# A decode kernel whose final wait for its two output stores is moved from SP to GpSimd

## The chip, the cores and the metric

The kernel runs on one core of one Trainium2 chip. The metric is the device time of one execution in microseconds (us). Every execution also has a span, from the first to the last recorded instruction. This change is far smaller than 2%, so the document leans on two finer quantities: the time of a run minus its span, and the records of one trace in nanoseconds (ns).

## The reference

One decode step of a transformer layer for a batch of 4: layer norm, attention over the last 4096 positions of a cache (32 query heads, 16 key and value heads of width 128), output projection and residual; then layer norm, a gated feed-forward block of width 4608 and residual. Everything is bf16.

```python
h = x + _A_ref(_layernorm(x, axis=-1), A_k_cache, A_v_cache, A_wq, A_wo)
h2 = h + _B_ref(_layernorm(h, axis=-1), B_W_gate, B_W_up, B_W_down)
return h2                       # 4 x 1 x 576, bf16
```

## The kernel before

The kernel keeps one list of operations for each engine. An operation names what it depends on; at the end each list is written out for its engine, and every dependency becomes a wait on a semaphore. An operation without a function (`None`) is only its waits. It becomes one instruction that waits, which the profile shows as an `EVENT_SEMAPHORE` at the helper's line L110.

```python
    for key, val in need.items():
        if seen.get(key, 0) < val:
            seen[key] = val
            engine.wait_ge(sems[key], val)          # L110
    if o.fn is None:
        continue
```

GpSimd prepares constants at the start (memsets and masks) and has nothing to do afterwards. SP issues every large load. The end of the kernel is this:

```python
dve("OUT0", lambda e: e.tensor_copy(out=out_sb[0:32, :], in_=bank[0][0:32, 0:288]), [("DOWN", 0)])
act("OUT1", lambda e: e.copy(out=out_sb[32:64, :], in_=bank[1][32:64, 0:288]), [("DOWN", 1)])
orow = out.rearrange("b s d -> (b s) d")
for n in range(2):
    P.dma(("sync", "scalar")[n], ("O", n), lambda e, n=n: e.dma_start(     # store n, L712
        out=orow[:, 288 * n:288 * n + 288], in_=out_sb[32 * n:32 * n + 4, :]),
        "d_out", [f"OUT{n}"])
P.op("sync", None, None, [("O", n) for n in range(2)])                     # the final wait
P.emit(nc, es)
```

SP issues one store and ACT the other. Both raise the semaphore `d_out` by 16 when they have landed, and the final wait is for 32.

Of the kernel before, what the change touches and what calls it, by code (L numbers as in the profile page):

```python
# [120 lines left out]
def bass_sequential_preLN__sliding_block_cached__glu_gated_reglu__decode_kernel(  # L121
# [12 lines left out]
    with ExitStack() as es:  # L134
# [5 lines left out]
        P = Prog()  # L140
# [104 lines left out]
        def main_rows(W):  # L245
            return W[0:512, :].rearrange("(p r) n -> p (r n)", r=4)
# [22 lines left out]
        for g, W in ((0, B_W_gate), (1, B_W_up)):  # L269
            for m, n, src in ((4, F // 2, last_rows(W)), (0, 3 * F, main_rows(W)[:, 0:3 * F]), (3, F, main_rows(W)[:, 3 * F:4 * F])):  # L270
                if g == 0 and m == 0:
                    n, src = 4 * F, main_rows(W)
# [438 lines left out]
        for n in range(2):  # L711
            P.dma(("sync", "scalar")[n], ("O", n), lambda e, n=n: e.dma_start(  # L712
                out=orow[:, 288 * n:288 * n + 288], in_=out_sb[32 * n:32 * n + 4, :]),
                "d_out", [f"OUT{n}"])
        P.op("sync", None, None, [("O", n) for n in range(2)])
        P.emit(nc, es)


# [26 lines left out]
```

## Time and profile before

| what | value | where it is read |
|---|---|---|
| time, median of the runs | 378.07 us (378.06, 378.07, 379.07) | the runs |
| span | 376.6 us | page, first line |
| DMA | mean 424 GB/s | page, part 2 |
| chain that ended last | 56% DMA, 21% PE, 20% DVE | page, part 4 |
| last 35 us of the span | one DMA piece of 32.31 us to 374.00 us | chain of waits |
| from the end of SP's wait to the last record of all | 1.461 us | raw trace |

These are lines of the page of the kernel before: its span, the DMA rows of part 2 (40 equal slices of the span) and the head of part 4, the chain that ended last.

```profile
span 376.6 us, 2562 instructions
...
DMA  8999999999999999999999999999999999999996
...
DMA packets 6802, 159.74 MB, mean 424 GB/s; under 512 B 764, under 2 KB 904, under 8 KB 1672
...
DMA 56%; PE 21%; DVE 20%; issue 1%; SPq 1%; ACT 0%
```

The digit 9 in almost every slice says that the DMA engines were busy 90% of the time or more. So the loads fill almost the whole span.

This is the end of the chain of waits of the kernel before, in order of time: start, length (us), what.

```profile
341.69 32.31 DMA sb_arena<-in_B_W_down_dram
374.00 0.04 issue
374.04 0.70 PE psb L705 x6
374.74 0.43 DVE sb_out_sb L708
```

The chain stops at VectorE's cast, at about 375.2 us. Behind it lies the part that this change touches. This is the timeline of the same kernel's tail: start, length (us), engine, line, operation. A `q` after an engine's name stands for its sequencer.

```profile
374.73 0.45 DVE L708 CAST sb_out_sb<-psb 32x288 bf16<-32x288 f32 x1 [9.73 <-PE psb L705]
374.76 0.39 ACT L709 CAST sb_out_sb<-psb 32x288 bf16<-32x288 f32 x1 [9.49 <-PE psb L705]
375.18 0.28 ACTq L712 DMA_DIRECT2D out_dram<-sb_out_sb  x1
375.20 0.34 SPq L712 DMA_DIRECT2D out_dram<-sb_out_sb  x1
```

The final wait is not in this view. It stands in the view of line L110, which gives durations in ns (least, median, most) and the first and last start in us, and in the view of what the SP queue waited for (us in total, times, longest):

```profile
L110 ACTq EVENT_SEMAPHORE  x13: 17/17/556, 20.9 to 334.5; - x13
L110 SPq EVENT_SEMAPHORE  x1: 17/17/17, 376.6 to 376.6; - x1
```

```profile
SPq L110 <- DMA out_dram<-sb_out_sb: 1.0, 1, 1.0
```

SP is done issuing its store and then waits 1.0 us for the stores to land. The 17 ns are only the record of a wait that is already over. The Trainium skill ("Perfetto Trace Analysis", Per-engine timelines, the part on sequencer-only instructions) says the same: the time spent in a semaphore wait is not in the record. This trace agrees for SP's wait, with 17 ns of record for 1.0 us of waiting. It does not agree for an instruction that waits for two semaphores: the longest of ACT's records above, 556 ns from 20.915 us, names two, of which one had its last update at 12.190 us and the other at 21.444 us, 27 ns before the record ended. The wait for the second is inside the record.

What follows the span is in no view, but the raw trace holds the updates of the semaphores. The next fence gives, in ns from the start of the span, the updates of semaphore 2, which no line of the kernel uses. A number in brackets is the step from the update before.

```
kernel before
SP's final wait                              376570 to 376587, end of the span
closing barrier, 9 updates                   374903 375818 375857 375901 376708 376752 376790 376824 376872
                                                    (915)   (39)   (44)  (807)   (44)   (38)   (34)   (48)
235 other semaphores, one update each        376828 to 377467
second barrier, 9 updates                    377691 ... 378048
                                                    (34)   (38)   (44)   (23)   (99)   (38)   (35)   (46)
```

I read each series of nine as a barrier, a place that no engine passes before all five have arrived: one pass over the five engines and back. The fifth update, from which the pass goes back, is called the turn below. The second barrier, where nobody is late, shows the undisturbed steps. The large steps in the first show who was late: the 807 ns end 121 ns after SP's wait. The last update minus 0.18 us is the time of the profiled run (378.048 against 377.87), so what happens behind the span counts in the metric.

### The profile page before, as it was taken

The numbers are of one execution on the slowest core, as the hardware profiler recorded it, in microseconds if no ns is written. First come the engines' busy times: TensorE is split into PE (matmuls) and PEld (weight loads), VectorE is DVE, ScalarE is ACT, GpSimd is POOL, SyncE is SP. The second block draws the span as 40 slices with busy tenths as digits, with TensorE's granted clock in tenths as the row PEclk, the third lists the DMA queues.
The fourth block names the chain that finished last, engine by engine and source line by source line (L and its number), as shares of the span: only waits on it lengthen the run. The fifth ranks groups of instructions, "written<-read, shape, count | busy, mean of one in ns | idle before, by whom it ended". The sixth has DMA issues, their size and how long they took to land.

```text
span 376.6 us, 2562 instructions
## 1 busy us (share of the span) xinstructions
PE 208.8 (55%) x1456; PEld 37.6 (10%) x703; DVE 226.2 (60%) x164; ACT 54.3 (14%) x85; POOL 10.5 (3%) x29
## 2 busy tenths in 40 slices
PE   0304443249919191749282845664655687886674
PEld 0000000001101010001010100100000001002422
DVE  3078888779292959584847777665659423333220
ACT  3193000301000114010101140101010401112010
POOL 8200000000000000000000000000000000000000
PEclk9955888859968797687788796989696968998699
DMA  8999999999999999999999999999999999999996
GB/s 335 446 439 428 416 442 439 428 418 442 437 425 421 439 440 421 421 442 442 425 419 439 442 428 418 438 439 428 425 435 439 423 425 439 422 431 425 437 413 260
DMA packets 6802, 159.74 MB, mean 424 GB/s; under 512 B 764, under 2 KB 904, under 8 KB 1672
## 3 DMA queue, kind: packets, MB, share of 16 engines
q1 hardware_dynamic: 6776, 159.59, 98.8%
q8 instruction: 8, 0.13, 0.1%
q10 hardware_dynamic: 16, 0.01, 0.0%
q14 instruction: 2, 0.02, 0.0%
HBM read 159.58 MB, written 0.00 MB: 424 GB/s over the span
## 4 chain that ended last, share of the span: by engine, by line
DMA 56%; PE 21%; DVE 20%; issue 1%; SPq 1%; ACT 0%
DMA sb_arena<-in_A_k_cache_dram 48%; DVE sb_arena L425 16%; PE psb L34 13%; DMA sb_arena<-in_B_W_down_dram 9%; PE psb L449 4%; PE psb L510 3%; DVE sb_o_tmp L523 1%; DVE sb_pp L488 1%; PE psb L476 1%; SPq L284 0%; DVE sb_pp L471 0%; DVE sb_hx L454 0%; ACT sb_pp L468 0%; PE psb L705 0%; DVE sb_out_sb L708 0%
## 5 line engine op out<-in xcount | busy, mean ns | idle before, releaser
L425 DVE STREAM_TRANSPOSE sb_arena<-sb_arena 128x8192 f32<-128x8192 f32 (+1 forms) x19 | 139.9, 7365 | 66.4 <-DMA sb_arena<-in_A_k_cache_dram 66.4
L449 PE MATMUL psb<-sb_arena 128*32 128x512 bf16 x256 | 44.5, 640 | 118.8 <-DVE sb_arena L425 118.8
L34 PE MATMUL psb<-sb_arena,sb_pp 128*128 128x512 bf16 x382 | 107.3, 389 | 2.9 <-issue 2.8
L510 PE MATMUL psb<-sb_arena,sb_pp 128*128 128x512 bf16 x115 | 44.8, 389 | 8.9 <-DVE sb_o_tmp L523 8.9
L34 PE MATMUL psb<-sb_arena 128*32 128x512 bf16 x256 | 45.4, 645 | 0.0
L520 ACT COPY sb_o_tmp<-psb 32x512 f32<-32x512 f32 x32 | 18.5, 577 | 181.7 <-PE psb L34 181.4
L523 DVE TENSOR_TENSOR sb_o_tmp<-psb,sb_fm 32x512 f32<-32x512 f32 x32 | 21.7, 678 | 18.6 <-PE psb L34 18.1
L449 PEld LDWEIGHTS psb<-sb_arena 128*32 128x32 bf16 x256 | 9.7, 117 | 162.0 <-DVE sb_arena L425 131.8
L510 PEld LDWEIGHTS psb<-sb_arena,sb_pp 128*128 128x128 bf16 x128 | 12.8, 100 | 115.7 <-issue 115.7
L527 DVE TENSOR_REDUCE sb_o_sel<-sb_o_tmp 128x128 f32<-128x512 f32 x16 | 17.7, 1107 | 0.5
L468 ACT ACTIVATE sb_pp<-psb,sb_hx 128x1024 bf16<-128x1024 f32 x4 | 4.5, 1113 | 79.4 <-DVE sb_hx L465 79.4
L488 DVE TENSOR_TENSOR sb_pp<-psb,sb_m 128x1024 bf16<-128x1024 f32 x8 | 9.3, 1206 | 4.6 <-PE psb L476 4.6
L483 ACT ACTIVATE sb_pp<-psb,sb_m 128x512 bf16<-128x512 f32 x16 | 9.8, 698 | 14.6 <-PE psb L476 14.6
L526 DVE TENSOR_TENSOR sb_o_tmp<-sb_o_tmp,sb_fm 64x512 f32<-64x512 f32 x16 | 11.0, 689 | 0.5
L416 ACT COPY sb_arena<-sb_q_keep 32x256 bf16<-32x256 bf16 x8 | 9.7, 1448 | 0.1
L402 DVE CAST sb_pp<-psb 128x512 bf16<-128x512 f32 x1 | 2.4, 2425 | 10.1 <-PE psb L382 10.1
L471 DVE STREAM_TRANSPOSE sb_pp<-sb_pp 128x1024 bf16<-128x1024 bf16 x4 | 5.0, 1245 | 5.1 <-ACT sb_pp L468 5.1
L476 PE MATMUL psb<-sb_pp,sb_to_v 128*32 128x256 bf16 x64 | 4.3, 400 | 6.2 <-DVE sb_pp L471 6.2
L705 PE MATMUL psb<-sb_arena,sb_pp 128*32 128x288 bf16 x72 | 5.4, 288 | 3.8 <-DMA sb_arena<-in_B_W_down_dram 3.8
L708 DVE CAST sb_out_sb<-psb 32x288 bf16<-32x288 f32 x1 | 0.4, 446 | 9.7 <-PE psb L705 9.7
L454 DVE TENSOR_REDUCE sb_hx<-psb 128x1 f32<-128x1024 f32 x4 | 4.9, 1225 | 2.3 <-PE psb L34 2.3
L34 PE MATMUL psb<-sb_arena,sb_hnT 128*32 128x384 bf16 x80 | 6.3, 394 | 0.0
(123 smaller groups left out, 80.4 us busy)
## 6 DMA issues: line engine op xcount, KB each, us to landing
sb_arena<-in_A_k_cache_dram SPq DMA_DIRECT2D x16, 4096.0 KB, 26.1
sb_arena<-in_A_v_cache_dram SPq DMA_DIRECT2D x16, 4096.0 KB, 28.6
sb_arena<-in_A_wo_dram SPq DMA_DIRECT2D x1, 4608.0 KB, 25.3
sb_arena<-in_B_W_gate_dram SPq DMA_DIRECT2D x1, 4608.0 KB, 26.9
sb_arena<-in_A_wq_dram SPq DMA_DIRECT2D x1, 4096.0 KB, 13.1
sb_arena<-in_B_W_down_dram SPq DMA_DIRECT2D x3, 1296.0 KB, 30.9
sb_arena<-in_B_W_up_dram SPq DMA_DIRECT2D x1, 3456.0 KB, 27.8
sb_arena<-in_B_W_up_dram SPq DMA_DIRECT2D x1, 1152.0 KB, 30.3
```

Of the source, the lines that this page charges most:

```text
L34: return e.add_instruction(mybir.InstMatmult(name=e.bass.get_next_instruction_name(), engine=mybir.EngineType.PE, ins=[e.lower_ap(rhs), e. ...
L416: act("QW", lambda e, i=i, q=q: e.copy(out=bass.AP(tensor=arena, offset=32 * i * AW + 2 * i + q, ap=[[AW, 32], [512, 16], [136, 4], [32, 4]]),
L425: dve(("TRA", g), lambda e: e.transpose(out=dst, in_=src), [("L", "K", g)] if lo == 0 else [])
L449: fn = lambda e, out_=out_, lhsT=lhsT, rhs=rhs, start=start, stop=stop: e.matmul(out_, lhsT=lhsT, rhs=rhs, start=start, stop=stop, skip_gr ...
L476: pe(("RM", b, n // 2), lambda e, n=n, i=i: e.matmul(bank[6 if n < 2 else 0][32 * i:32 * i + 32, n % 2 * 256:n % 2 * 256 + 256], lhsT=to_v ...
L483: act(("EV", b, 0), lambda e, a=a: e.activation(out=bass.AP(tensor=pp, offset=2 * a, ap=[[PPW, 128], [8, 2], [32, 128], [1, 2]]), in_=bank ...
L488: dve(("EV", b, 1), lambda e, n=n: e.tensor_tensor(out=bass.AP(tensor=pp, offset=16 + 8 * n, ap=[[PPW, 128], [32, 128], [2, 4], [1, 2]]), ...
L510: fn = lambda e, lhsT=lhsT, rhs=rhs, k=k, j=j: e.matmul(bank[2 + j], lhsT=lhsT, rhs=rhs, start=(k == 0), stop=(k == 7), skip_group_check=True)
L520: act(("OSC", g), lambda e, j=j: e.copy(out=o_tmp[32 * j:32 * j + 32, 0:512], in_=bank[2 + j][32 * j:32 * j + 32, :]), [("PV", g), ("OSEL" ...
L523: dve(("OSD", g), lambda e, j=j: e.tensor_tensor(out=ot(32 * j, 32), in0=bank[2 + j][32 * j:32 * j + 32, :].rearrange("p (t d) -> p t d", ...
L526: dve(("OS", g), lambda e: e.tensor_tensor(out=ot(64, 64), in0=ot(64, 64), in1=fmb(64, 64), op=ALU.mult), [("OSC", g)])
L527: dve(("OSEL", g), lambda e: e.tensor_reduce(out=o_sel[:, qd, b, :], in_=o_tmp[:, 0:512].rearrange("p (t d) -> p d t", d=DH), axis=AX.X, o ...
```

## The change

The final wait leaves SP's list and goes to the end of GpSimd's. It is still the same wait: the kernel may not end before both stores have landed. The diff has no comment; its intent, as I read it, is to let an engine that is idle since 12 us do the waiting, and to end SP's program with its store.

```diff
-        P.op("sync", None, None, [("O", n) for n in range(2)])
+        P.op("gpsimd", None, None, [("O", n) for n in range(2)])
```

No other instruction of any engine moves.

## The prediction

> **What bounds the kernel.** The page's DMA row reads 8 or 9 tenths in nearly every slice, at a mean of 424 GB/s. The chain that ended last is 56% DMA. In the last 40 us it is one DMA piece (the W_down load, 32.31 us to 374.00), then PE 0.70 us and a VectorE cast of 0.43 us to about 375.2. GpSimd works only in the first 12 us (its timeline).
>
> **What the change does.** Every listed instruction keeps its place on its engine. One semaphore wait for both output stores leaves SP's queue and goes behind GpSimd's last memset. Nothing before 375.2 us depends on it, so no load, buffer release or matmul moves.
>
> **The tail, from the raw records of the trace (us from the span's start).**
> - The stores are issued at 375.18 (ACT) and 375.20 (SP).
> - The stores' semaphore counts up until 376.553. SP's wait begins its 17 ns record at 376.570 and the span ends at 376.587.
> - After that, semaphore 2 shows the closing barrier. Its nine updates are at 374.903, 375.818, 375.857, 375.901, 376.708, 376.752, 376.790, 376.824 and 376.872. Then semaphores are reset, and a further barrier ends at 378.048.
>
> The Trainium skill ("Runtime: NRT & Kernel Launch", The ~15µs preamble/postamble breakdown) lists a postamble barrier, reset and barrier, and describes the opening barrier as a serpentine of 8 hops at 44 ns. The trace agrees: nine updates, and hops of 34 to 48 ns where nobody is late. I read the order, as inference from the times, as PE, ACT, GpSimd, VectorE, SP and back. The 807 ns before the fifth update is the wait for SP, at the turn.
>
> **Cost.** Before: from the end of the wait to VectorE's returning update takes 121 + 44 = 165 ns. After: GpSimd is released at the same moment, two places ahead of the turn. It needs its own time to its update, then the hop to VectorE (44 ns), then VectorE out to VectorE back (about 135 ns, from the undisturbed opening barrier: 24 + 111). I estimate GpSimd's own time at 150 ns, from SP's 121 ns plus the some 30 ns by which it seems slower from barrier to first reset. This is 329 ns against 165 ns. So I expect about +0.16 us, all on the critical path.
>
> The runs before are 378.06, 378.07 and 379.07 us, so one run's spread (1 us) is larger than the effect (0.04%).
>
> **Prediction: 378.2 us, 8 in 10 between 377.6 and 379.1. Faster by over 2%: 0.01; within 2%: 0.98; slower by over 2%: 0.01.**
>
> **What would show the steps.** Right: the last record is GpSimd's wait, at 376.6 within the run's own DMA drift; the SP queue has no wait for the output stores; the chain of waits, DMA row and busy times are unchanged; in the barrier's updates the third, not the fifth, is the late one; and from the end of the wait to the last barrier update takes 1.5 to 1.8 us, against 1.46 us now (378.048 - 376.587). Wrong: that tail is unchanged or shorter, or the fifth update is still the late one.
>
> **What could make it wrong.** GpSimd may wake or leave its program more slowly than SP (ACT took 0.354 us from its store issue's end to its update): up to +0.4 us. My reading of the barrier's order may be wrong. Drift of the 375 us of loads by a few tenths can hide or reverse the sign in a median of three. Over 2% would need the loads to move.

## The result

The changed kernel takes 378.50 us (median of 4 runs, 378.44 to 378.65), beside 378.06 us for the kernel before (4 runs, 378.00 to 379.07). The ratio is 1.0006 with a 95% interval of 0.9989 to 1.0023. A ratio is the mean time of one kernel's fast runs over that of the other's of the same rounds, so it is not quite the ratio of the medians: the one run of 379.07 us raises the mean of before.

The same lines of the page of the changed kernel:

```profile
span 376.6 us, 2577 instructions
...
DMA  8999999999999999999999999999999999999996
...
DMA packets 6802, 159.74 MB, mean 424 GB/s; under 512 B 764, under 2 KB 904, under 8 KB 1672
...
DMA 61%; DVE 18%; PE 18%; SPq 1%; issue 0%
```

The span, the DMA row and the rate are as before. The shares of the chain are not quite (DMA 61% against 56%): more of its earlier pieces are loads of the key cache, 53% of the span against 48%. (The 15 more instructions are matmul records, 1471 against 1456, of which a trace can miss some.) The end of its chain of waits has the same steps, 0.05 us later:

```profile
342.56 31.49 DMA sb_arena<-in_B_W_down_dram
374.05 0.04 issue
374.09 0.70 PE psb L705 x6
374.79 0.43 DVE sb_out_sb L708
```

In its view of line L110, SP's row is gone and GpSimd has one. The SP queue's waits contain no line for the output stores any more.

```profile
L110 POOLq EVENT_SEMAPHORE  x1: 17/17/17, 376.6 to 376.6; - x1
```

Nothing in the profile's views is longer, and yet the run is 0.4 us longer. The difference is in the raw records behind the span:

```
kernel after
GpSimd's final wait                          376627 to 376644, end of the span
closing barrier, 9 updates                   374955 375864 377186 377230 377253 377350 377389 377425 377471
                                                    (909) (1322)   (44)   (23)   (97)   (39)   (36)   (46)
second barrier, 9 updates                    378262 ... 378620
```

Now the third update is the late one, and all that follow have the steps of a barrier where nobody else is late. So GpSimd is third, as the prediction had inferred. But its update comes 377186 - 376644 = 542 ns after the end of its wait, where SP's came after 121 ns. From the end of the span to the last update it is 1.976 us instead of 1.461 us: 0.515 us more. Of these, 421 ns are the slower exit (542 against 121), 121 ns the longer way from the third place than from the fifth (285 against 164 ns to the barrier's end), and 27 ns are won back behind the barrier.

### The profile page after: what moved, and what is told of

The parts are those of the page before. It is cut to its first block, busy times and chain, and to the rows that moved or that the text cites. A ratio compares the mean times of both kernels' runs of the same rounds, so it can differ in the third digit from the quotient of the medians.

```text
span 376.6 us, 2577 instructions
## 1 busy us (share of the span) xinstructions
PE 209.9 (56%) x1471; PEld 36.0 (10%) x703; DVE 226.3 (60%) x164; ACT 54.3 (14%) x85; POOL 10.5 (3%) x29
## 4 chain that ended last, share of the span: by engine, by line
DMA 61%; DVE 18%; PE 18%; SPq 1%; issue 0%
DMA sb_arena<-in_A_k_cache_dram 53%; DVE sb_arena L425 16%; PE psb L34 11%; DMA sb_arena<-in_B_W_down_dram 8%; PE psb L449 4%; PE psb L510 3%; DVE sb_o_tmp L523 1%; DVE sb_pp L488 1%; SPq L284 0%; SPq L242 0%; PE psb L476 0%; PE psb L705 0%; DVE sb_out_sb L708 0%; SPq L255 0%; SPq L251 0%
## 5 line engine op out<-in xcount | busy, mean ns | idle before, releaser
L449 PE MATMUL psb<-sb_arena 128*32 128x512 bf16 x256 | 41.6, 625 | 120.8 <-DVE sb_arena L425 120.8
L34 PE MATMUL psb<-sb_arena,sb_pp 128*128 128x512 bf16 x384 | 107.6, 390 | 0.0
L510 PE MATMUL psb<-sb_arena,sb_pp 128*128 128x512 bf16 x128 | 50.6, 395 | 8.9 <-DVE sb_o_tmp L523 8.9
L34 PE MATMUL psb<-sb_arena 128*32 128x512 bf16 x256 | 42.8, 639 | 0.0
L449 PEld LDWEIGHTS psb<-sb_arena 128*32 128x32 bf16 x256 | 8.7, 120 | 163.4 <-DVE sb_arena L425 133.9
L34 PE MATMUL psb<-sb_arena,sb_hnT 128*32 128x384 bf16 x80 | 7.2, 446 | 0.0
L676 DVE TENSOR_TENSOR sb_pp<-psb,sb_pp 128x384 bf16<-128x384 f32 x3 | 1.5, 550 | 8.8 <-PE psb L667 8.8
```

The source lines that it names most:

```text
L34: return e.add_instruction(mybir.InstMatmult(name=e.bass.get_next_instruction_name(), engine=mybir.EngineType.PE, ins=[e.lower_ap(rhs), e. ...
L449: fn = lambda e, out_=out_, lhsT=lhsT, rhs=rhs, start=start, stop=stop: e.matmul(out_, lhsT=lhsT, rhs=rhs, start=start, stop=stop, skip_gr ...
L510: fn = lambda e, lhsT=lhsT, rhs=rhs, k=k, j=j: e.matmul(bank[2 + j], lhsT=lhsT, rhs=rhs, start=(k == 0), stop=(k == 7), skip_group_check=True)
```

## The experiments

Three theories stood at the start.

- **Exit theory**: GpSimd always takes over 0.5 us from its program's last instruction to its update in the closing barrier, and it stands two places ahead of the turn. Both are paid because everything behind the last engine to arrive is serial.
- **Wake theory**: GpSimd was slow because it had been parked in a wait for 364 us.
- **Drift theory**: the difference of the times came from the loads, and the tail had no part in it.

In what follows, "exit" is the time from the end of an engine's last record to its own update in the closing barrier, "tail" is the time from the end of the span to the last update of the second barrier, both from the trace of the profiled run, and "run minus span" is the median over the runs (spans are noted to 0.1 us). The kernel before ran nine times beside each batch: medians 377.96, 378.04 and 377.88 us, and a run minus span of 1.26, 1.26 and 1.27 us. The 95% interval of each ratio is about 0.13% (some 0.5 us) wide to either side, so smaller differences below rest on run minus span and on the records, not on the ratio. Each batch ran on another chip.

### The changed kernel again

No edit.

> The changed kernel again, beside the kernel before on one chip. Tail theory: run time minus span, which was 1.3 us before and 1.8 us after, is again about 0.5 us longer than for the kernel before, and the time is 0.4 to 0.6 us longer. Drift theory (the difference came from the loads): run time minus span is alike and the difference of the times changes size or sign.

Measured: 378.51 us against 377.96 us, ratio 1.0013 (1.0001 to 1.0026). Run minus span is 1.84 us in the median, and lies between 1.81 and 1.84 us in all five runs; for the kernel before it lies between 1.22 and 1.32 us in all nine. Exit 542 ns and tail 1.976 us, the same to the nanosecond as in the first trace. The spans are alike (376.6 to 376.8 us here; 376.5 to 376.7 us before, but for one of 377.3). The drift theory falls: the loss of about 0.55 us is real and lies behind the span. The first comparison showed 0.44 us.

### Both wait

```diff
         P.op("sync", None, None, [("O", n) for n in range(2)])
+        P.op("gpsimd", None, None, [("O", n) for n in range(2)])
```

> The wait is added on GpSimd and kept on SP. If only the engine that is late at the barrier counts, SP's own wait is hidden behind GpSimd's: same time as the changed kernel (about 378.5 us), third barrier update about 540 ns after GpSimd's wait record ends. If taking the wait from SP had itself cost or saved something, the time differs from the changed kernel by over 0.1 us.

Measured: 378.55 us, exit of GpSimd 542 ns, tail 1.974 us. The view of line L110 shows the two waits, which end 8 ns apart:

```profile
L110 SPq EVENT_SEMAPHORE  x1: 17/17/17, 376.8 to 376.8; - x1
L110 POOLq EVENT_SEMAPHORE  x1: 17/17/17, 376.8 to 376.8; - x1
```

So the half of the change that frees SP gains nothing: with SP's wait put back, the time is the changed kernel's. All of the loss is in the half that makes GpSimd wait.

### A second wait on GpSimd, meant to wake it shortly before

```diff
-        P.op("sync", None, None, [("O", n) for n in range(2)])
+        P.op("gpsimd", None, None, ["OUT0"])
+        P.op("gpsimd", None, None, [("O", n) for n in range(2)])
```

> GpSimd waits first for VectorE's output cast (about 375.2 us) and then for the stores, so it has been parked for only some 1.4 us when the stores land. Wake theory (the 542 ns come from having been parked 364 us): the time from its last wait record to its barrier update falls to about 150 ns and the total to about 378.1 us. Exit theory (GpSimd always needs about 540 ns to leave its program): 500 to 580 ns again and about 378.5 us.

```profile
L110 POOLq EVENT_SEMAPHORE  x1: 42/42/42, 376.6 to 376.6; - x1
```

Measured: 378.59 us. The record ends at 376.673 us and the update is at 377.216 us: 543 ns. But the edit did not do what it was meant to do. GpSimd has one record and not two; it names both semaphores, begins at 376.631 us, 24 ns after the last landing of the stores, and lasts 42 ns. The cast had been over since 375.242 us. If it had woken GpSimd for a second wait inside this instruction, the record should hold that wait of some 1.4 us, as ACT's record of 556 ns held its second wait. So this run shows no early waking, and it leaves the wake theory open. The two runs below in which SP waits and GpSimd works decide it.

### The wait on ACT

```diff
-        P.op("sync", None, None, [("O", n) for n in range(2)])
+        P.op("scalar", None, None, [("O", n) for n in range(2)])
```

> The wait is on ACT, second in my reading of the barrier's order. Position and exit theory: the second update is the late one, the third and fourth follow it by 39 and 44 ns, the turn takes about 24 + 100 ns; the time is longer than the kernel before by its place (two hops of about 40 ns, the hop to SP and a turn some 60 ns longer, about 0.1 to 0.15 us) plus what ACT's own exit exceeds SP's 121 ns. If ACT leaves as fast as SP: about 378.2 us; if it needs the 354 ns seen after its store issue: about 378.5 us.

Measured: 378.04 us (before: 377.96), run minus span 1.40 us, tail 1.581 us. The second update is the late one, as the order said, and the exit is 109 ns. ACT stands farther from the turn than GpSimd and still costs only about 0.1 us, so the place explains little; the exit does. The 354 ns from the end of ACT's store issue to its update, which the prediction had taken as a warning, are not what ACT needs after a wait; whether they belong to leaving right behind a store issue is not tested.

### The wait on VectorE

The same edit with `"vector"`.

> The wait is on VectorE, one place before the turn in my reading. The fourth barrier update is the late one; the fifth follows 24 ns and the sixth 97 ns later. If VectorE leaves its program as fast as SP and ACT (121 and 109 ns), the tail from the end of the wait to the last barrier update is 1.50 to 1.58 us and the time 0.05 to 0.15 us over the kernel before. If a slow exit is common to the compute engines and ACT is the exception, the tail is about 1.9 us.

Measured: the fourth update is the late one, exit 147 ns, tail 1.534 us: as expected. The time, 378.31 us against 378.04 us, is not: 0.27 us longer, and run minus span is 1.60 us. The profiled run (379.26 us, in a span that was itself 1 us longer) ended 0.05 us after the last barrier update, where all the other traces so far, before and after included, have it 0.17 to 0.18 us before that update. About 0.23 us lie outside everything that the barrier's records show. One of the later experiments takes this up.

### The wait on PE

The same edit with `"tensor"`.

> The wait is on PE, first in my reading: the first update is the late one and all others follow it at 34, 38, 44, 24, 97, 38, 35 and 47 ns. Place theory: 34 ns more than on ACT plus the difference of the exits. PE's exit is not known; from its 196 ns between the end of its last matmul and its update I expect 100 to 250 ns, so a tail of 1.61 to 1.76 us and a time of 0.15 to 0.35 us over the kernel before. About 1.6 us of tail would say PE leaves like ACT.

Measured: 378.21 us against 378.04 us, the first update is the late one, exit 192 ns, tail 1.720 us. All inside what was expected.

### GpSimd waits and then works

```diff
-        P.op("sync", None, None, [("O", n) for n in range(2)])
+        pool("end", lambda e: e.memset(warm[:, 0:1], 0.0), [("O", n) for n in range(2)])
```

> GpSimd waits for the stores and then does one memset of a column (98 ns elsewhere). If the 542 ns are counted from GpSimd's last instruction of its program, the third update comes 98 to 160 ns later than in the changed kernel (0.64 to 0.70 us after the wait's end). If they are counted from the wait and a memset hides in them, it stays at about 0.54 us. If the memset has the engine finish what a bare wait leaves to the exit, it shrinks below 0.5 us.

This is the memset in the timeline of that run; the bracket says that GpSimd had idled 364.57 us until the stores landed:

```profile
376.77 0.10 POOL L715 MEMSET sb_warm<- 128x1 f32 x1 [364.57 <-DMA out_dram<-sb_out_sb]
```

Measured: the memset ends at 376.873 us and the update is at 377.385 us, 512 ns later, and 659 ns after the stores' last landing (376.726 us), against 583 ns in the changed kernel (376.603 to 377.186). So 76 of the memset's 99 ns are paid on top, and the exit is counted from the last instruction. After a memset it is 30 ns shorter than after a bare wait. The time of 379.06 us (4 runs) doesn't say more, because two of the runs had a span of 377.7 us; run minus span is 1.76 us.

### SP waits, and GpSimd works too long

```diff
+        pool("late", lambda e: e.memset(oT[:, 0:32, :], 0.0), ["OUT0", "OUT1"])
+        pool("late2", lambda e: e.memset(arena[:, 0:512], 0.0), ["late"])
         P.op("sync", None, None, [("O", n) for n in range(2)])
```

> The wait stays on SP as in the kernel before, but GpSimd does two memsets (about 0.95 and 0.5 us) after the output casts, which end near 376.75 us. Exit theory: GpSimd is late at the barrier although nobody moved the wait; its update comes 0.45 to 0.6 us after the last memset's end, at about 377.3 us, and the run takes 0.5 to 0.75 us longer than the kernel before. If the slow exit belongs to a GpSimd that had to wait for a semaphore last, its update comes some 0.15 us after the memset (376.9 us) and the run is 0.2 to 0.3 us longer.

The two added memsets in the timeline, and the rows of the two waits in the view of line L110 (GpSimd's is here the wait for ACT's cast; the first memset itself carries the wait for VectorE's):

```profile
375.38 0.96 POOL L715 MEMSET sb_oT<- 128x1024 bf16 x1 [362.95 <-DVE sb_out_sb L708]
376.40 0.53 POOL L716 MEMSET sb_arena<- 128x512 bf16 x1
```

```profile
L110 POOLq EVENT_SEMAPHORE  x1: 17/17/17, 375.3 to 375.3; - x1
L110 SPq EVENT_SEMAPHORE  x1: 17/17/17, 376.7 to 376.7; - x1
```

Measured: 378.58 us against 378.04 us, with the wait on SP as in the kernel before. GpSimd's last memset ends at 376.921 us and its update comes 518 ns later, at 377.439 us. SP's wait was over at 376.689 us. The exit belongs to GpSimd leaving its program, whatever it did last. The wake theory falls here: GpSimd had been awake since 375.3 us and at work for 1.5 us, and its exit was as slow. What stays untested is a GpSimd that is busy through the whole kernel; in all these runs it had been idle for some 363 us when the tail began.

### SP waits, and GpSimd works a little

```diff
+        pool("late", lambda e: e.memset(oT[:, 0:8, :], 0.0), ["OUT0", "OUT1"])
         P.op("sync", None, None, [("O", n) for n in range(2)])
```

> SP keeps the wait, and GpSimd does one memset of 256 columns after the output casts, which ends near 375.6 us. Exit theory with slack: its update comes about 0.52 us later, at 376.15 us, before SP is done (376.7 us), so the time is that of the kernel before within 0.05 us and run time minus span is 1.26 us. If late work on GpSimd costs by itself, the time rises by 0.1 us or more.

```profile
375.27 0.32 POOL L715 MEMSET sb_oT<- 128x256 bf16 x1 [362.99 <-DVE sb_out_sb L708]
```

That line is of its timeline. Measured: 377.90 us against 377.88 us, run minus span 1.27 us. The memset ends at 375.592 us, the update follows at 376.109 us (517 ns), and SP's, the fifth, is at 376.708 us. The wake theory fails here too: the last thing that GpSimd did was not a wait of 364 us but 0.32 us of work. The same exit costs nothing where another engine arrives later: 377.90 us here, 378.58 us when the work ended 1.3 us later.

### A drain between the wait and the exit

```diff
-        P.op("sync", None, None, [("O", n) for n in range(2)])
+        pool(None, lambda e: e.drain(), [("O", n) for n in range(2)])
```

> GpSimd waits for the stores and then executes one drain (a record of its own, on an engine that has had nothing to do for 364 us). If a drain is a dear instruction on GpSimd, its record lasts 150 to 400 ns, against 7 to 10 ns on the other engines in the opening, and the exit's 542 ns may hold one of that kind. If the 186 ns of GpSimd's drain in the opening were only the memsets in flight, the record lasts under 30 ns and the exit's cost lies elsewhere. The third update comes later than 0.54 us after the wait by the drain and its issue, unless the drain does the exit's work in advance: then it stays near 0.54 us.

Measured: 378.47 us. The drain carries the wait itself and has the only record; it lasts 41 ns (376.650 to 376.691 us, between the two forecasts), and the update comes 529 ns after it. One drain is not dear on an idle GpSimd (the 186 ns in the opening stand behind memsets that are still running), and it doesn't do the exit's work in advance. What GpSimd does in the half microsecond stays open: the trace has no record there.

### SP waits, and VectorE has one instruction more

```diff
+        P.op("vector", None, None, ["OUT1"])
         P.op("sync", None, None, [("O", n) for n in range(2)])
```

> SP keeps the final wait; VectorE gets one more instruction at the end of its program, a wait for ACT's output cast that is over at 375.2 us. With the wait on VectorE the run time exceeded the span by 1.60 us where the barrier's records explain 1.36 us, and the trace showed one more 8 KB fetch of instructions before the start. If that excess comes with VectorE's longer program: run time minus span is 1.45 to 1.55 us here (1.26 in the kernel before) with a tail of 1.46 us, and the run is about 0.23 us longer. If it comes with VectorE being late: 1.26 us, and no change.

Measured: 378.16 us against 377.88 us, run minus span 1.52 us, tail 1.438 us, with SP's update as the late one, 127 ns after the end of its wait. VectorE is not late at the barrier at all, and still the run is some 0.25 us longer (run minus span is 1.46 to 1.56 us in the five runs, and 1.23 to 1.28 us in the nine before); again it ends 0.05 us after the last barrier update. So the unexplained part of the run with the wait on VectorE comes with VectorE's program having one instruction more, and not with VectorE arriving late. Its cause is open: no record shows where the time goes. Fetches of instructions, which the expectation mentions, don't follow it: the traces show six of the 8 KB kind in this run, nine in the run with the drain, which has no such excess, and eight in the kernel before.

### The five exits together

| final wait on | place in the order | exit, ns | tail, us | run minus span, us |
|---|---|---|---|---|
| PE | 1 | 192 | 1.720 | 1.55 |
| ACT | 2 | 109 | 1.581 | 1.40 |
| GpSimd (the change) | 3 | 542 | 1.976 | 1.84 |
| VectorE | 4 | 147 | 1.534 | 1.60 (0.23 of it not in the tail) |
| SP (before) | 5 | 121 | 1.461 | 1.26 |

Each tail is the exit plus the undisturbed steps behind that place plus the reset and the second barrier. For ACT: 109 + (38 + 44 + 24 + 97 + 38 + 36 + 47) + 791 + 357 = 1581 ns, where 791 ns lie between the two barriers and 357 ns are the second. The gap between the barriers lay between 787 and 819 ns in all the traces, and the two later traces with SP as the late engine gave tails of 1.431 and 1.438 us, so the tails are good to some 0.03 us. SP has the shortest way: it stands at the turn, and its exit is among the short ones. Of the five places for this wait the kernel before has the shortest tail, so the experiments point to no version that beats both kernels.

## Why the prediction was right or wrong

The forecast of the time was right: 378.2 us with a range of 377.6 to 379.1, and 378.50 us was measured. The mechanism was right too, but its size was not: the forecast rise of 0.16 us was measured as 0.44 us and, beside the kernel before on one chip, as 0.55 us. That the time still fell into the range is owed to the width of the range. Point by point:

- **The loads do not move.** Right. Span and DMA row are equal in both profiles, and the end of the chain of waits has the same steps.
- **The order of the barrier** (PE, ACT, GpSimd, VectorE, SP and back), inferred from times. Right: with the wait on PE, ACT, GpSimd, VectorE and SP, the first, second, third, fourth and fifth update is the late one.
- **"all on the critical path"**, and nothing gained on SP. Right: with both engines waiting the time is the changed kernel's (378.55 us).
- **"I estimate GpSimd's own time at 150 ns"**. Wrong: it is 542 ns. This is the term that was mis-sized. The sum of 329 ns (150 + 44 + 135) measured 706 ns (542 + 44 + 120), against 165 ns before. That makes 541 ns; the tail grew by 515 ns, as the gap between the two barriers was 28 ns shorter than in the trace of before. The two later traces with SP as the late engine have the shorter gap (791 ns) as well.
- **"from the end of the wait to the last barrier update takes 1.5 to 1.8 us"**. Wrong for the same reason: 1.976 us.
- **"up to +0.4 us"** for a slow GpSimd. The risk was named, and the text can be read in two ways. As the whole rise it is too small: about 0.55 us, by the medians of five and nine runs on one chip. On top of the 0.16 us it fits: GpSimd's exit was 0.39 us above the estimate (542 against 150 ns).
- **What made the time fit nevertheless**: the range allowed for 1 us of spread between runs, and the first comparison showed only 0.44 us of the loss.

The estimate failed because it was taken from another engine (SP) and from another event, GpSimd's first semaphore reset behind the barrier. The trace of before could not show GpSimd's exit: GpSimd left its program near 12 us and stood at the barrier long before it counted.

## What to carry to other kernels

In this kernel the last wait belonged on the engine from whose arrival the least was left to do, exit and way through the barrier together. That was SP, and an idle engine was not a free one, because GpSimd took 0.51 to 0.54 us to get from its last instruction to the barrier. The same exit cost nothing when another engine arrived later (377.90 against 377.88 us), so end GpSimd's work early and let it not be last. What is at stake is half a microsecond, here of 378. When two profiles agree in every view and the times don't, compare the time minus the span, and then the semaphore updates behind the span.

## What the Trainium skill lacked or had wrong

- "Runtime: NRT & Kernel Launch", The ~15µs preamble/postamble breakdown, gives the closing barrier, the reset and the second barrier with DMA rearm as about 1.5, 1.5 and 2 us. In the kernel before the whole way from the end of the last wait to the last barrier update took 1.46 us: 0.29 us to the barrier's end, writes to the semaphores from 376.83 to 377.47 us, and 0.36 us for the second barrier's updates. (The page's first figure includes waiting for the engines, and no record here shows a DMA rearm, so the sums do not cover quite the same.) The figure of 44 ns a hop and 355 ns for a barrier agrees (steps of 23 to 99 ns, 357 ns in all), but the steps are not equal: the turn at SP took 97 to 99 ns.
- The same page does not say in which order the engines pass the barrier (PE, ACT, GpSimd, VectorE, SP and back, shown by making each of them late), nor what an engine needs to reach it: 109 ns on ACT, 121 on SP, 147 on VectorE, 192 on PE and 512 to 543 on GpSimd.
- "GPSIMD Engine Reference" describes what dispatch and completion of an instruction consist of, but not what leaving a program costs; the 0.51 to 0.54 us stood behind a wait, a memset and a drain alike.
- "Perfetto Trace Analysis", Per-engine timelines, leaves the wait for semaphores out of the record of a sequencer-only instruction. With two semaphores the wait for the second was inside it: 556 ns on ACT, against 17 ns where one was waited for.
- No page that was read has an explanation for the some 0.25 us that a run took longer when VectorE's program had one wait more (378.16 against 377.88 us), with nothing of it in the barrier's records.
